# The first MoE's weight preparation spread over three engines, and batch 0's scores read from whole q and k

## The chip, the cores and the metric

The kernel runs on one core of one Trainium2 chip. The metric is device time in microseconds (us), as the median of several executions. The core has five engines that matter here: TensorE (PE in the rows, with PEld for its weight loads), VectorE (DVE), ScalarE (ACT), GpSimd (POOL) and SyncE (SP), whose queue issues most DMAs. Each engine works through its own instructions in the order in which they were written; an instruction that has to wait holds up everything behind it on that engine.

## The reference

Three stages follow one another: attention (the sum of a full attention over q, k and v averaged four by four, and of a local one in which a position sees the 3 before and the 3 behind it), a first MoE with one activation, and a second MoE with a product of two projections.

```python
    q_d = q.reshape(B, H, Sd, factor, D).mean(axis=3)      # k_d, v_d alike
    out_d = sm_attn(q_d, k_d, v_d)
    out_up = np.repeat(out_d, factor, axis=2)
    mask = np.abs(pos[:, None] - pos[None, :]) < factor
    ...
    out_local = np.matmul(attn, v)
    return (out_up + out_local).astype(np.float32)
...
    h = x @ w_in                # first MoE: 2304 x 512 by 512 x 2048
    r = np.maximum(h, 0.0)
    g = s * (r * r) + b
    return (g @ w_out).astype(np.float32)
...
    a = x @ w_a                 # second MoE: 512 x 1536, twice
    b = x @ w_b
    return (a * b @ w_out).astype(np.float32)
```

There are 4 batches of 576 positions, 8 heads of 64. The weights of both MoEs arrive as 64-bit floats.

## The kernel before, in words

**Order.** The kernel is a list of tasks. Each has an engine, a modelled duration, inputs, buffers that it takes and gives back, and a due time. `Program.order` (a list scheduler inside the kernel file) takes again and again the task that can start first, and among equals the one that is due first, and writes the instructions in that order. So the order of each engine's instructions is fixed when the kernel is built; on the chip only semaphores hold. `SEEN` is the modelled delay from the end of a task until another engine sees it. An engine named `GQ` stands for DMAs that GpSimd issues; in the emitted program these DMAs (line 541) are instructions of GpSimd's own stream. Due times are counted from `T0` and `STEP` (`target(idx)` is the due time of iteration idx of the first MoE) with the constants `DUE_...`.

**Attention, in four steps a part.** `down(b, hp)` is the averaged attention of batch b and head pair hp: q and k are loaded whole (128 x 576), averaged (line 572 on VectorE for batch 0, lines 574 and 575 on GpSimd for the others), scores on TensorE (L610), softmax on VectorE and ScalarE, transposes (L661), the product with the averaged v (L681). For batch 0, v is averaged by lines 595 and 596 on GpSimd; for the others `pool_in` sums it by DMAs that accumulate (L541), three for each half, each behind the one before. `tile_job(i)` is the local attention of 96 positions by TensorE (scores L760 on q and k loaded for the tile, transposes L810, product L828, sum with the upsampled part L842, split into high and low L493 and L497). Eight tiles, of positions 0 to 767, are done this way; the others are `unit`s of 128 positions, done on VectorE (L879 to L955).

**The ramp.** The first 768 positions (batch 0's and batch 1's `down`, eight tiles) and the weights of the first MoE are the ramp. Its buffers are one pool (`rp`). The pool of the units is opened only when all ramp tasks are written (`open_b`), and takes its memory over.

**Weights.** `w_slice(k)` makes one of 32 slices (128 x 512) of the first MoE's weights. The raw 64-bit words come by DMA into one of 33 shared slots `w`. ScalarE makes z from the upper words (L334) and three bits of the lower words (L345); VectorE puts the sign there (L350) and joins both (L358). Then the value is split into two parts: the high one is rounded by ScalarE (L374), the low one is the difference, by VectorE (L379). At most `MAX_STAGED` raw slices are in SBUF at a time. Line 345 has four forms: it reads 16-bit or 8-bit elements and writes 32-bit or 16-bit ones, by turns.

**First MoE.** 6 blocks of 384 positions, 16 iterations each, 96 iterations. One iteration is 12 matmuls into h (L1030 to L1032), three ScalarE passes (L1047, L1051, L1054), one VectorE subtraction (L1058) and 12 matmuls into acc (L1073 to L1075). Iteration f of block 0 needs weight slices 2f and 2f+1 and block 0's positions (tiles 0 to 3). Block 1 needs tiles 4 to 7, block 2 three units. Until the first of these matmuls the kernel fills gaps on TensorE with small matmuls (L266) that keep its clock up; behind it there are no fillers.

**Second MoE.** From about 541 us to the end, on the result of the first. Its weights go through the same lines 334 to 358.

Of the kernel before, what the change touches and what calls it, by code (L numbers as in the profile page):

```python
# [7 lines left out]
F32 = mybir.dt.float32  # L8
# [3 lines left out]
U8 = mybir.dt.uint8  # L12
# [55 lines left out]
RAMP_BUFS = {"dq": 1, "dk": 1, "dv": 2, "qd": 1, "kd": 1, "vp": 4, "tq": 2, "tk": 2, "tv": 2, "e": 1, "x": 1, "z": 2}  # L68
# [6 lines left out]
ENGINES = ("PE", "DVE", "ACT", "POOL", "SP", "GQ", "CTL")  # L75

SEEN = {"PE": 0.2, "DVE": 0.13, "ACT": 0.22, "POOL": 0.15, "SP": 2.0, "GQ": 2.5, "CTL": 0.0}


class Task:  # L80
    __slots__ = (
        "eng", "dur", "fn", "deps", "succ", "acq", "picks", "rel", "due", "lead", "share", "num", "left", "ready", "start",
        "end", "fill",
# [24 lines left out]
class Program:  # L108
# [8 lines left out]
    def add(self, eng, dur, fn, reads=(), writes=(), acq=(), rel=(), due=1e9, after=(), lead=0.0, share=1.0):  # L117
        t = Task()
        t.eng, t.dur, t.fn, t.acq, t.rel, t.due = eng, dur, fn, acq, rel, due
# [14 lines left out]
    def order(self):  # L134
        for t in reversed(self.tasks):
            for s in t.succ:
                t.due = min(t.due, s.due - s.dur - SEEN[t.eng])
# [17 lines left out]
        while len(out) < len(self.tasks):  # L155
# [49 lines left out]
            for a in t.rel:  # L205
                a = a(t) if callable(a) else a
                self.free[a].append(t.end + SEEN[t.eng])
            out.append((t, picks))
            for u in t.succ:
                u.left -= 1  # L210
                u.ready = max(u.ready, t.end + (0.0 if u.eng == t.eng == "PE" else SEEN[t.eng]))
# [15 lines left out]
def moe_chain(ctx, tc, qT, kT, vd, tq, tk, tv, qu, ku, vu, w_a1, w_o1, w_a2, w_b2, w_o2, sb, ident_d, bmask_d, emask_d, out):  # L227
# [85 lines left out]
    def w_words(k, spool, z, first, name, acq=(), after=()):  # L313
# [49 lines left out]
    def w_slice(k, ph, lo_eng, after=()):  # L363
# [1268 lines left out]
```

## Time and profile before

| | us |
|---|---|
| median of 3 executions | 978.01 |
| lowest, highest | 977.96, 978.42 |
| the profiled execution | 977.19 |
| its span, from the first to the last instruction | 975.4 |

The page shows one execution. Busy time is what an engine spent inside instructions; a wait of an engine is named with the instruction that ended it. The table by stretches gives busy time of each engine between two times, with the granted TensorE clock (1.00 is 2.4 GHz, 0.50 is 1.2 GHz). TensorE's busy time before about 85 us holds the fillers, so it says little there.

### The profile page before, as it was taken

To read this page: it belongs to the slowest core of one execution; us is meant where nothing else is said; L and a number is where in the kernel's file an instruction comes from. 1 tells how busy PE (TensorE), PEld (TensorE's weight loads), DVE (VectorE), ACT (ScalarE), POOL (GpSimd) and SP (SyncE) were. 2 spreads that over 40 slices of the span, in tenths; PEclk is the share of its full clock that TensorE was granted. 3 is DMA by queue.
4 is the path that set the end of the run, shared out by engine and by line. 5 is a ranking of instruction groups with operands and counts; after the bars stand their busy time and mean duration, and the time that the engine had idled before them with its cause. 6 is when DMAs were issued, how large, how long until landed. Compare 5 with 4: busy or idle time off the path is not lost.

```text
span 975.4 us, 14509 instructions
## 1 busy us (share of the span) xinstructions
PE 930.3 (95%) x5371; PEld 858.5 (88%) x5371; DVE 787.2 (81%) x1377; ACT 520.4 (53%) x1144; POOL 76.7 (8%) x86
## 2 busy tenths in 40 slices
PE   8589699999899999999999999999999999999997
PEld 4357699999799999999999999998999998999995
DVE  5378888899999999997776899978977779777753
ACT  3479999434444454434888756534533334533322
POOL 2440110202222120000000000000000000000000
PEclk9799799999799999999999999999999999999999
DMA  6676851623435342321456623100500000200001
GB/s 181 151 231 201 275 165 44 199 78 89 147 106 100 121 121 66 98 65 51 164 169 230 229 72 124 64 22 23 173 22 23 22 22 11 98 22 23 0 1 66
DMA packets 48159, 99.19 MB, mean 102 GB/s; under 512 B 6536, under 2 KB 22248, under 8 KB 47704
## 3 DMA queue, kind: packets, MB, share of 16 engines
q1 hardware_dynamic: 40888, 95.60, 29.9%
q0 software_dynamic: 7200, 2.67, 2.4%
q8 instruction: 42, 0.69, 0.3%
q14 instruction: 29, 0.24, 0.1%
HBM read 85.65 MB, written 12.58 MB: 101 GB/s over the span
## 4 chain that ended last, share of the span: by engine, by line
PE 79%; DVE 9%; ACT 5%; DMA 3%; issue 2%; POOL 1%; SPq 0%; ACTq 0%; POOLq 0%
PE ab L1304 26%; PE h L1030 6%; PE h L1032 6%; PE acc L1073 6%; PE h L1031 6%; PE acc L1074 6%; PE acc L1075 6%; PE acc L1446 5%; PE acc L1445 5%; PE acc L1444 5%; DMA pv<-in_vd_dram 2%; ACT w L345 1%; DVE pr L940 1%; DVE xo L1181 1%; PE sc L610 1%
## 5 line engine op out<-in xcount | busy, mean ns | idle before, releaser
L1304 PE MATMUL ab<-xo,w 128*128 128x384 f32 x1370 | 276.9, 339 | 1.0 <-DVE w L1334 0.5
L1304 PEld LDWEIGHTS ab<-xo,w 128*128 128x128 f32 x1370 | 246.7, 189 | 16.9 <-DVE u L1378 0.8
L1030 PE MATMUL h<-xsh,w 128*128 128x384 f32 x384 | 132.8, 346 | 1.6 <-ACT u L1047 0.8
L1073 PE MATMUL acc<-gh,w 128*128 128x384 f32 (+1 forms) x384 | 132.5, 345 | 0.5 <-ACT w L345 0.5
L1074 PE MATMUL acc<-gl,w 128*128 128x384 f32 x384 | 130.3, 339 | 0.7 <-DVE gl L1058 0.7
L1032 PE MATMUL h<-xsh,w 128*128 128x384 f32 x384 | 130.4, 340 | 0.2 <-DVE w L379 0.2
L1031 PE MATMUL h<-xsl,w 128*128 128x384 f32 x384 | 130.4, 340 | 0.0
L1075 PE MATMUL acc<-gh,w 128*128 128x384 f32 (+1 forms) x384 | 129.9, 338 | 0.0
L1047 ACT ACTIVATE u<-h 128x384 f32<-128x384 f32 x96 | 48.1, 501 | 123.2 <-PE h L1032 118.3
L1420 ACT ACTIVATE gh<-u 128x384 fp32r<-128x384 f32 x68 | 35.8, 526 | 90.5 <-DVE u L1381 54.4
L1030 PEld LDWEIGHTS h<-xsh,w 128*128 128x128 f32 x384 | 73.3, 191 | 4.8 <-issue 2.3
L1073 PEld LDWEIGHTS acc<-gh,w 128*128 128x128 f32 x384 | 72.5, 189 | 2.6 <-issue 1.3
L1074 PEld LDWEIGHTS acc<-gl,w 128*128 128x128 f32 x384 | 72.6, 189 | 1.6 <-DVE gl L1058 1.6
L1032 PEld LDWEIGHTS h<-xsh,w 128*128 128x128 f32 x384 | 73.2, 191 | 0.6 <-DVE w L379 0.6
L1031 PEld LDWEIGHTS h<-xsl,w 128*128 128x128 f32 x384 | 73.3, 191 | 0.0
L1075 PEld LDWEIGHTS acc<-gh,w 128*128 128x128 f32 x384 | 72.5, 189 | 0.0
L1058 DVE TENSOR_TENSOR gl<-u,gh 128x384 fp32r<-128x384 f32 x96 | 54.0, 562 | 16.8 <-ACT gh L1054 16.5
L1328 ACT ACTIVATE w<-ab 128x384 f32<-128x384 f32 x32 | 15.7, 491 | 92.9 <-PE ab L1304 89.0
L345 ACT ACTIVATE w<-w 128x512 int32<-128x512 uint8 (+3 forms) x63 | 63.6, 1025 | 0.0
L350 DVE TENSOR_SCALAR w<-w 128x512 uint16<-128x512 f32 x63 | 47.5, 765 | 14.2 <-ACT w L345 14.0
L1054 ACT ACTIVATE gh<-u 128x384 fp32r<-128x384 f32 x96 | 50.6, 528 | 2.4 <-PE acc L1075 0.4
L1051 ACT ACTIVATE u<-u 128x384 f32<-128x384 f32 x96 | 50.7, 528 | 1.9
(199 smaller groups left out, 1790.2 us busy)
## 6 DMA issues: line engine op xcount, KB each, us to landing
w<-in_w_o_dram SPq DMA_DIRECT2D x27, 512.0 KB
w<-in_w_a_dram SPq DMA_DIRECT2D x26, 512.0 KB
bk<-in_ku_dram SPq DMA_DIRECT2D x22, 320.0 KB
bk<-in_vu_dram SPq DMA_DIRECT2D x22, 320.0 KB
w<-wod SPq DMA_DIRECT2D x12, 512.0 KB
w<-in_w_b_dram SPq DMA_DIRECT2D x10, 512.0 KB
dk<-in_kT_dram SPq DMA_DIRECT2D x16, 288.0 KB
x2d<-ev SPq DMA_DIRECT2D x24, 192.0 KB
```

The source lines that it names most:

```text
L345: A_.activation(out=halves()[:, :, 0] if k % 2 else low, in_=src, func=ACTF.Copy, scale=scale, bias=bias)
L1030: nc.tensor.matmul(out=st["h"], lhsT=w[:, 0, k], rhs=hi[:, k], start=(k == 0), stop=False)
L1031: nc.tensor.matmul(out=st["h"], lhsT=w[:, 0, k], rhs=lo[:, k], start=False, stop=False)
L1032: nc.tensor.matmul(out=st["h"], lhsT=w[:, 1, k], rhs=hi[:, k], start=False, stop=(k == HP - 1))
L1051: A_.activation(out=st["u"], in_=st["u"], func=ACTF.Square)
L1054: A_.activation(out=st["hi"][:, :n], in_=st["u"], func=ACTF.Copy)
L1058: V.tensor_tensor(out=st["lo"], in0=st["u"], in1=st["hi"][:, :n].bitcast(F32), op=ALU.subtract)
L1073: nc.tensor.matmul(out=acc, lhsT=wh, rhs=st["hi"], start=(f == 0), stop=False)
L1074: nc.tensor.matmul(out=acc[:, :n], lhsT=wh, rhs=st["lo"], start=False, stop=False)
L1075: nc.tensor.matmul(out=acc, lhsT=wl, rhs=st["hi"], start=False, stop=(f == FA - 1))
L1304: nc.tensor.matmul(out=o, lhsT=w[:, k], rhs=x, start=(not more and k + n == 0), stop=(k == 1 and n == 2), skip_group_check=more,)
L1444: nc.tensor.matmul(out=acc, lhsT=gh, rhs=w[:, 0], start=first, stop=False)
```

## The change

1. **q and k of batch 0** are loaded into `w` slots (8 of them) and stay until all six tiles of batch 0 have their scores. These tiles read them there, and their own loads of q and k are gone (12 loads).
2. **v of batch 0** is averaged on VectorE (one reduction for each of 8 halves) instead of two GpSimd instructions each.
3. **The accumulating DMAs** belong to GpSimd in the scheduler, too, with 6.0 us until they are seen; `GQ` is gone. They and batch 1's `down` are due later.
4. **Line 345** has one form left: 16-bit in, 32-bit out. This holds for all 68 slices of both MoEs.
5. **High parts** of the first MoE's 32 slices go from ScalarE to VectorE (a copy); **every second low part** goes from VectorE to GpSimd.
6. `MAX_STAGED` is 5 instead of 3, buffer counts of the ramp, due times and leads are other numbers.

```diff
-W_ENG_A = ["DVE"]
+W_ENG_A = ["DVE", "POOL"]
+
+H_ENG_A = ["DVE"]
 DOWN_ENG = [("DVE", "DVE")] * 4
-MAX_STAGED = 3
+MAX_STAGED = 5
...
-T0, STEP = 36.0, 3.95 / 384
-LEAD = 20.0
-DUE_DOWN = (12.0, 2.5, 0.0, 8.0)
-DUE_TILE = (4.0, 5.0, 25.0)
-DUE_JOB = (14.0, 12.0, 15.0)
+T0, STEP = 28.8, 3.759 / 384
+LEAD = 10.0
+DUE_DOWN = (8.8, -5.0, 0.0, 8.0)
+DUE_NEXT = (46.5, 0.0)
+DUE_TILE = (12.1, 11.0, 18.5)
+DUE_JOB = (14.0, 19.5, 21.0)
...
-RAMP_BUFS = {"dq": 1, "dk": 1, "dv": 2, "qd": 1, "kd": 1, "vp": 4, "tq": 2, "tk": 2, "tv": 2, "e": 1, "x": 1, "z": 2}
+RAMP_BUFS = {"dq": 2, "dk": 2, "dv": 2, "qd": 1, "kd": 1, "vp": 4, "tq": 1, "tk": 1, "tv": 2, "e": 1, "x": 1, "z": 2}
...
-ENGINES = ("PE", "DVE", "ACT", "POOL", "SP", "GQ", "CTL")
-
-SEEN = {"PE": 0.2, "DVE": 0.13, "ACT": 0.22, "POOL": 0.15, "SP": 2.0, "GQ": 2.5, "CTL": 0.0}
+ENGINES = ("PE", "DVE", "ACT", "POOL", "SP", "CTL")
+
+SEEN = {"PE": 0.2, "DVE": 0.13, "ACT": 0.22, "POOL": 0.15, "SP": 2.0, "CTL": 0.0}
...
             low = st["low"] = words()[:, :, 0]
-            if k % 4 < 2:
-                src, scale, bias = halves()[:, :, 1], 2.0 ** -13, -4095.5 * 2.0 ** -13
-            else:
-                src = st["s"].rearrange("p a m -> p (a m)").bitcast(U8).rearrange("p (m c) -> p m c", c=8)[:, :, 3]
-                scale, bias = 2.0 ** -5, -15.5 * 2.0 ** -5
-            A_.activation(out=halves()[:, :, 0] if k % 2 else low, in_=src, func=ACTF.Copy, scale=scale, bias=bias)
-
-        add("ACT", 0.9, a_fn, [("st", k)], [("low", k)])
+
+            A_.activation(out=low, in_=halves()[:, :, 1], func=ACTF.Copy, scale=2.0 ** -13, bias=-4095.5 * 2.0 ** -13)
+
+        add("ACT", 0.56, a_fn, [("st", k)], [("low", k)])
...
-            A_.activation(out=wt[k][:, 0], in_=st["z"], func=ACTF.Copy)
-
-        add("ACT", 0.52, h_fn, [("t", k)], [("wh", k)], [("w",)])
+            if h_eng == "DVE":
+                V.tensor_copy(out=wt[k][:, 0], in_=st["z"])
+            else:
+                A_.activation(out=wt[k][:, 0], in_=st["z"], func=ACTF.Copy)
+
+        add(h_eng, 0.35 if h_eng == "DVE" else 0.52, h_fn, [("t", k)], [("wh", k)], [("w",)])
...
-        add(lo_eng, 1.23 if lo_eng == "POOL" else 0.61, l_fn, [("wh", k)], [("w", k)], rel=[ph + "z"])
+        add(lo_eng, 1.33 if lo_eng == "POOL" else 0.61, l_fn, [("wh", k)], [("w", k)], rel=[ph + "z"])
...
+    def wide_in(p):
+        return slot(p[0], F32).rearrange("p a m -> p (a m)")[:, :S]
...
-                    "GQ" if r else "SP", 1.3, fn, (), [("pv", b)] if r == 3 else (), () if r + kh else [("pv",)], (), due,
-                    [t[kh]] if r else [t[0]] if kh else after,
+                    "POOL" if r else "SP", 1.25, fn, (), [("pv", b)] if r == 3 else (), () if r + kh else [("pv",)], (), due,
+                    [t[kh]] if r else [t[0]] if kh else after, seen=6.0,
...
-            st["k"] = new(ph, "dk", [128, S])
+            st["k"] = whole["k", b, hp] = wide_in(p) if b == 0 else new(ph, "dk", [128, S])
...
-        load(l_q, 128 * HP * TQ * 4, writes=[("tq", i)], acq=[(names["tq"],)], after=after)
-        load(l_k, 128 * HP * TW * 4, writes=[("tk", i)], acq=[(names["tk"],)], after=after)
+        if b:
+            load(l_q, 128 * HP * TQ * 4, writes=[("tq", i)], acq=[(names["tq"],)], after=after)
+            load(l_k, 128 * HP * TW * 4, writes=[("tk", i)], acq=[(names["tk"],)], after=after)
+
+        k0, k1 = max(0, 3 - t0), min(TW, S + 3 - t0)
...
+                add("CTL", 0.0, free_fn, after=mm["whole"], rel=["w"] * 2 * HP)
...
-        down(0, hp, "r", DOWN_ENG[hp], "POOL", target(0) - DUE_DOWN[0] + DUE_DOWN[1] * hp)
+        down(0, hp, "r", DOWN_ENG[hp], "DVE", target(0) - DUE_DOWN[0] + DUE_DOWN[1] * hp)
...
-        w_slice(k, "r", W_ENG_A[k % len(W_ENG_A)])
-    pool_in(1, P.made["open", "r"], target(0))
+        w_slice(k, "r", H_ENG_A[k % len(H_ENG_A)], W_ENG_A[k % len(W_ENG_A)])
+    pool_in(1, P.made["open", "r"], target(FA) - DUE_NEXT[0])
     for hp in range(HP):
-        down(1, hp, "r", ("POOL", "POOL"), "POOL", target(0))
+        down(1, hp, "r", ("POOL", "POOL"), "POOL", target(FA) - DUE_NEXT[0] + DUE_NEXT[1] * hp)
```

## Rows read from the trace of the kernel before

**Rows 1.** The page's first part: busy time, share of the span, instructions, by engine.
```profile
PE 930.3 (95%) x5371; PEld 858.5 (88%) x5371; DVE 787.2 (81%) x1377; ACT 520.4 (53%) x1144; POOL 76.7 (8%) x86
```

**Rows 2.** Table by stretches: from:to, length, busy time of each engine, PEclk, DMA.
```profile
0.00:34.40 34.40, 26.35 (x190) 14.66 (x190) 18.74 (x46) 15.36 (x75) 9.81 (x17) 0.95 0.62 173
34.40:45.30 10.90, 4.27 (x28) 2.50 (x29) 0.01 (x1) 0.66 (x3) 6.68 (x10) 0.59 0.57 111
45.30:60.00 14.70, 10.64 (x97) 7.48 (x98) 8.63 (x19) 8.56 (x41) 5.87 (x9) 0.84 0.70 199
60.00:170.60 110.60, 100.17 (x721) 88.01 (x718) 93.97 (x187) 108.12 (x268) 15.12 (x14) 0.95 0.59 184
...
174.20:254.50 80.30, 75.18 (x444) 72.35 (x443) 77.64 (x107) 36.68 (x84) 13.51 (x13) 0.98 0.43 132
254.50:541.00 286.50, 286.31 (x1699) 277.94 (x1698) 247.97 (x373) 161.93 (x345) 25.76 (x25) 0.99 0.39 120
```

**Rows 3.** Waits from 0 to 60 us: who waited for whom, total, times, longest.
```profile
PE o L681 <- POOL vp L596: 13.9, 4, 7.7
```

**Rows 4.** GpSimd in order of time, 38 to 41 us: start, length, instruction.
```profile
38.02 1.21 POOL L541 DMA_DIRECT2D pv<-in_vd_dram  x1 [3.32 <-issue]
...
40.07 0.45 POOL L596 TENSOR_TENSOR vp<-dv 72x128 f32<-72x128 f32 x1
```

**Rows 5.** The accumulating DMAs, line 541, 0 to 180 us: issue to landing.
```profile
DMA to landing us min/median/max: 3.7/5.9/10.9
```

**Rows 6.** TensorE in order of time: first MoE's start, a stall, ends of blocks 0 and 1.
```profile
84.68 0.44 PE L1030 MATMUL h<-xsh,w 128*128 128x384 f32 x1
...
104.75 1.92 PE L828 MATMUL o<-w,tv 102*64 102x96 f32 x16 [6.81 <-ACT w L820]
...
107.81 0.52 PE L1031 MATMUL h<-xsl,w 128*128 128x384 f32 x1
108.13 0.52 PE L1032 MATMUL h<-xsh,w 128*128 128x384 f32 x1
...
170.08 0.33 PE L1032 MATMUL h<-xsh,w 128*128 128x384 f32 x1
...
253.01 0.67 PE L1030 MATMUL h<-xsh,w 128*128 128x384 f32 x1
```

**Rows 7.** VectorE in order of time: the last low part, the first unit.
```profile
169.90 0.69 DVE L379 TENSOR_TENSOR w<-z,w 128x512 fp32r<-128x512 f32 x1 [0.15 <-ACT w L374]
...
174.19 2.03 DVE L879 TENSOR_TENSOR pr<-bq,bk 128x1792 f32<-128x1792 f32 x1 [1.46 <-DMA bq<-in_qu_dram]
```

**Rows 8.** Groups of instructions by form: count, busy time, mean ns of one.
```profile
L345 ACT ACTIVATE w<-w 128x512 uint16<-128x512 uint8 x16 | 21.9, 1372 | 0.0
L379 DVE TENSOR_TENSOR w<-z,w 128x512 fp32r<-128x512 f32 x32 | 21.9, 691 | 1.4 <-ACT w L374 1.1
L374 ACT ACTIVATE w<-z 128x512 fp32r<-128x512 f32 x32 | 20.5, 648 | 0.3 <-DVE z L358 0.3
L345 ACT ACTIVATE w<-w 128x512 int32<-128x512 uint16 x15 | 10.3, 689 | 0.0
```

**Rows 9.** VectorE's two converting copies, in order of time.
```profile
4.87 0.32 DVE L293 CAST bmaskb<-tq 96x306 bf16<-96x306 f32 x1 [3.78 <-DMA tq<-in_bmask_dram]
...
11.41 0.21 DVE L288 CAST identb<-ident 96x96 bf16<-96x96 f32 x1 [1.94 <-DMA ident<-in_ident_dram]
```

**Rows 10.** GpSimd sums in order of time: two lengths, then one beside VectorE's work.
```profile
57.32 0.67 POOL L574 TENSOR_TENSOR dq<-dq 128x288 f32<-128x288 f32 x1
58.07 0.44 POOL L575 TENSOR_TENSOR qd<-dq 128x144 f32<-128x144 f32 x1
...
68.17 2.05 POOL L574 TENSOR_TENSOR dq<-dq 128x288 f32<-128x288 f32 x1
```

**Rows 11.** VectorE in order of time: one instruction alone, then beside GpSimd's sums.
```profile
46.51 1.00 DVE L802 TENSOR_TENSOR w<-w,tsm 96x816 f32<-96x816 f32 x1
...
50.98 1.72 DVE L802 TENSOR_TENSOR w<-w,tsm 96x816 f32<-96x816 f32 x1
```

More of the change, by code (lines that the diff above doesn't have):

```diff
@@ L11 @@
 I32 = mybir.dt.int32
-U8 = mybir.dt.uint8
 U16 = mybir.dt.uint16
@@ L82 @@
         "eng", "dur", "fn", "deps", "succ", "acq", "picks", "rel", "due", "lead", "share", "num", "left", "ready", "start",
-        "end", "fill",
+        "end", "fill", "seen",
     )
@@ L115, in __init__, with add @@
         self.free = {k: [0.0] * n for k, n in free.items()}
-    def add(self, eng, dur, fn, reads=(), writes=(), acq=(), rel=(), due=1e9, after=(), lead=0.0, share=1.0):
+    def add(self, eng, dur, fn, reads=(), writes=(), acq=(), rel=(), due=1e9, after=(), lead=0.0, share=1.0, seen=None):
         t = Task()
+        t.seen = SEEN[eng] if seen is None else seen
         t.eng, t.dur, t.fn, t.acq, t.rel, t.due = eng, dur, fn, acq, rel, due
@@ L136, in order @@
             for s in t.succ:
-                t.due = min(t.due, s.due - s.dur - SEEN[t.eng])
+                t.due = min(t.due, s.due - s.dur - t.seen)
         avail = {e: [] for e in ENGINES}
@@ L206, in order @@
                 a = a(t) if callable(a) else a
-                self.free[a].append(t.end + SEEN[t.eng])
+                self.free[a].append(t.end + t.seen)
             out.append((t, picks))
@@ L210, in order @@
                 u.left -= 1
-                u.ready = max(u.ready, t.end + (0.0 if u.eng == t.eng == "PE" else SEEN[t.eng]))
+                u.ready = max(u.ready, t.end + (0.0 if u.eng == t.eng == "PE" else t.seen))
                 if not u.left:
@@ L361, in w_words, with w_slice @@
         return tz
-    def w_slice(k, ph, lo_eng, after=()):
+    def w_slice(k, ph, h_eng, lo_eng, after=()):
         st = {}
@@ L527, in moe_chain @@
     pooled = {}
+    whole = {}
+    def wide_in(p):
+        return slot(p[0], F32).rearrange("p a m -> p (a m)")[:, :S]
     def pool_in(b, after, due):
@@ L555, in l_k @@
         def l_k(p):
-            st["k"] = new(ph, "dk", [128, S])
+            st["k"] = whole["k", b, hp] = wide_in(p) if b == 0 else new(ph, "dk", [128, S])
             return st["k"], kT[b, hp]
         def l_q(p):
-            st["q"] = new(ph, dq, [128, S])
+            st["q"] = whole["q", b, hp] = wide_in(p) if b == 0 else new(ph, dq, [128, S])
             return st["q"], qT[b, hp]
-        load(l_k, 128 * S * 4, writes=[("dk", key)], acq=[(ph + "dk",)], after=after)
-        load(l_q, 128 * S * 4, writes=[("dq", key)], acq=[(ph + dq,)], after=after)
+        load(l_k, 128 * S * 4, writes=[("dk", key)], acq=[("w",) if b == 0 else (ph + "dk",)], after=after)
+        load(l_q, 128 * S * 4, writes=[("dq", key)], acq=[("w",) if b == 0 else (ph + dq,)], after=after)
         for name, src in (("k", "dk"), ("q", "dq")):
@@ L578, in down @@
                 eng, dve(S) if eng == "DVE" else 1.25, prep, [(src, key)], [(name + "d", key)],
-                [(ph + name + "d",)], [ph + (dq if src == "dq" else src)],
+                [(ph + name + "d",)], [ph + (dq if src == "dq" else src)] if b else (),
             )
@@ L745, in l_v, with qk @@
             return st["v"], tv[i]
-        load(l_q, 128 * HP * TQ * 4, writes=[("tq", i)], acq=[(names["tq"],)], after=after)
-        load(l_k, 128 * HP * TW * 4, writes=[("tk", i)], acq=[(names["tk"],)], after=after)
+        if b:
+            load(l_q, 128 * HP * TQ * 4, writes=[("tq", i)], acq=[(names["tq"],)], after=after)
+            load(l_k, 128 * HP * TW * 4, writes=[("tk", i)], acq=[(names["tk"],)], after=after)
+        k0, k1 = max(0, 3 - t0), min(TW, S + 3 - t0)
+        def qk(name, hp):
+            if b:
+                return st[name][:, hp] if name == "q" else st[name][:, hp, k0:k1]
+            w = whole[name, b, hp]
+            return w[:, t0:t0 + TQ] if name == "q" else w[:, t0 - 3 + k0:t0 - 3 + k1]
         load(l_v, TW * DM * 4, writes=[("tv", i)], acq=[(names["tv"],)], after=after)
@@ L760, in s_fn @@
                     nc.tensor.matmul(
-                        out=sc[h][:, hp], lhsT=st["q"][h * D:h * D + D, hp], rhs=st["k"][h * D:h * D + D, hp],
+                        out=sc[h][:, hp, k0:k1], lhsT=qk("q", hp)[h * D:h * D + D], rhs=qk("k", hp)[h * D:h * D + D],
                         start=False, stop=(hp == HP - 1),
@@ L765, in tile_job, with free_fn @@
         ts = add(
-            "PE", 1.75, s_fn, [("tq", i), ("tk", i), "const"], [("tsc", i)], [wide, wide, E_SLOT[ph]],
-            [names["tq"], names["tk"]], after=[mm["dS", b, hp] for hp in range(HP)], lead=LEAD, share=0.55,
-        )
+            "PE", 1.75, s_fn, ([("tq", i), ("tk", i)] if b else [(x, (0, hp)) for x in ("dk", "dq") for hp in range(HP)]) + ["const"],
+            [("tsc", i)], [wide, wide, E_SLOT[ph]], [names["tq"], names["tk"]] if b else (),
+            after=[mm["dS", b, hp] for hp in range(HP)], lead=LEAD, share=0.55,
+        )
+        if b == 0:
+            mm.setdefault("whole", []).append(ts)
+            if len(mm["whole"]) == S // TQ:
+                def free_fn(p):
+                    pass
+                add("CTL", 0.0, free_fn, after=mm["whole"], rel=["w"] * 2 * HP)
         def m_fn(p):
```

## The prediction

> **What bounds the kernel now.** I read the page's first part, then the table by stretches, then the waits of the first 60 us, and only then single instructions. The first part says that TensorE is busy for 95% of the span [rows 1], but its fillers count in that, so the table is the better view [rows 2]. From 254.5 to 541 us TensorE is busy 286.3 of 286.5 us: nothing can be won there but TensorE work, and the change takes none away. Before that three things are to be seen. From 34.4 to 45.3 us VectorE has 0.01 us of work and ScalarE 0.66, and the clock falls to 0.59: the whole ramp stands. From 60 to 170.6 ScalarE is busy 108.1 of 110.6 us (98%), VectorE 94.0 (85%): ScalarE sets the pace of the weights. From 174.2 to 254.5 VectorE is busy 77.6 of 80.3 us: it makes the three units on which block 2 waits.
>
> The standstill has a name. TensorE waits four times, 13.9 us in all, for line 596, the averaged v that GpSimd makes [rows 3]. In GpSimd's order that instruction stands behind an accumulating DMA that runs only at 38.0; v is done at 40.5 [rows 4]. These DMAs land 3.7 to 10.9 us after their issue, median 5.9 [rows 5], and each waits for the one before on the engine that also owes v to TensorE. The scheduler put them on an engine of their own, which the program does not have.
>
> The first MoE's matmuls start at 84.68, and block 0's last h ends at 170.4 [rows 6]. VectorE makes the last low part at 169.90 and only then starts the first unit, at 174.19, because the units' pool opens behind all of the ramp [rows 7]. Block 2 starts at 253.0 [rows 6], one VectorE stretch later. So the end of the ramp, pushed along by VectorE's full stretch and then by TensorE's full one, sets the end of the kernel. A microsecond off the ramp is a microsecond off the total.
>
> **The change part by part.** ScalarE in the ramp: 32 high parts of 648 ns leave it, 20.7 us. Of line 345's 32 instructions there, 16 write 16-bit elements at 1372 ns; they become the form of 689 ns, 16 x 0.68 = 10.9 us [rows 8]. That is 31.6 us of instruction lengths; busy time counts where two overlap once, so I take 25 us as the safe end. ScalarE stops being the bound: 108.1 less 25 is 83 us of 110.6. The other half of line 345 is in the second MoE, where TensorE is the bound; I count it at nothing, since TensorE's full stretch hides it.
>
> VectorE in the ramp: it is busy 18.7 + 0.0 + 8.6 + 94.0 = 121.4 us up to 170.6, and idle 49.2 [rows 2]. Sixteen low parts go: 16 x 0.69 = -11.0 us [rows 8]. The copies come: no copy of 512 elements is in the trace. The two converting copies took 0.32 us for 306 elements and 0.21 for 96 [rows 9], 0.52 ns an element, so 512 take 0.21 + 416 x 0.00052 = 0.43 us (an estimate), 13.7 us for 32. If the rounding copy runs at the rate of a subtraction it is 0.69 us, 22.1 us in all [rows 8]. I take 0.43, since a copy is nearer to a copy. Eight v averages come, each a reduction over 512 elements; a subtraction of 512 takes 0.69 us [rows 8], and at that rate they are 5.5 us.
>
> Sixteen low parts come to GpSimd. Its sums took 0.67 us for 288 elements and 0.44 for 144 with VectorE out of the way [rows 10], 1.6 ns an element, so 512 take about 1.0 us; beside VectorE's work the same 288 elements took 2.05 us [rows 10]. That is 16 to 50 us in a ramp of 150, on an engine that was busy 37.5 us up to 170.6 [rows 2] and drops sixteen v sums: it has room. What they cost VectorE is the open price. A product of two operands on VectorE went from 1.00 to 1.72 us beside GpSimd's sums [rows 11]; elsewhere it was GpSimd that waited, as in the 2.05 us. I take half of the 0.72, rounded down to 0.3 us for each of 16, 5 us, with 0 and 16 (each one holds VectorE for its whole 1.0 us) as the ends.
>
> Work for VectorE: 121.4 - 11.0 + 13.7 + 5.5 + 5 = 134.6 us. The ends are 128 (no contention) and 152 (slow copies, full contention).
>
> Idle time of VectorE: of the 49.2 us, the 10.9 of the standstill go, since v is now made where its consumers' other inputs are made, and about 4 of the 6.1 from there to 60 us go with them (6.2 of TensorE's 13.9 us for line 596 are outside its longest wait [rows 3]). Of the 15.7 idle up to 34.4, 5 are the first loads; with q and k no longer queued for one buffer each and five raw slices let in instead of three, weights can fill some of it. I keep 14 of these 17.8. From 60 on 16.6 were idle beside a full ScalarE; an engine that is the bound is held 98% busy by this kind of order, as ScalarE shows [rows 2], so I keep 4. Idle together 18, with 8 and 26 as ends.
>
> The ramp then ends at 134.6 + 18 = 152.6 instead of 170.6: 18.0 us earlier. TensorE can follow: it does the last 64 iterations and the rest of its attention in 286.5 us [rows 2], at most 4.5 us an iteration, so block 0 takes at most 72 us. What is late next is VectorE itself, in the ramp and then in the units; its stretch of 80 us before block 2 stays, and behind that TensorE's.
>
> Other edits. The twelve loads that go (tiles 0 to 5) free queue time on SyncE; the waits of the first 60 us name no such load as TensorE's releaser, so I count nothing beyond the idle time above. Eight `w` slots are held until the sixth tile's scores; of 33 slots that leaves 25 for weights, more than are ready by then, and if it did not, weight loads would wait on SyncE's queue and loads behind them as well. The accumulating DMAs are still instructions of GpSimd: each waits there for the one before, and low parts and batch 1's averages are queued behind it. With 6.0 us planned and 5.9 the median landing [rows 5], the wait is about nothing; at 10.9 it is 4.9 us for each of six, 29 us of GpSimd time, of which only a low part needed within that time reaches TensorE. The other due times, leads and buffer counts change the order alone; I have no row that prices them and let the range carry them, 5 us to either side.
>
> The sum against the profiled execution is 977.2 - 18.0 = 959.2; the median of the runs shown is 0.8 us above that execution, so 960.0.
>
> **The rivals.** (a) The ramp shrinks further. VectorE's low end with 8 us idle is 128 + 8 = 136, the ramp ends 34.6 us earlier, and the time is 943. For it speaks that no single engine was full before 60 us [rows 2]; against it that TensorE, VectorE and ScalarE hand each tile to and fro, and each hand-over waits. I give its whole region, 943 to 952, 0.20.
>
> (b) GpSimd holds VectorE up. Each of the 16 low parts shuts VectorE out for its whole length: 16.5 us instead of 5, and the time is 971.5; with a landing at 10.9 us in front of a needed low part it is up to 976. For it speaks the stretched product [rows 11], against it the sum of 2.05 us [rows 10]: there GpSimd waited. The chance is 0.17. The Trainium skill, "SBUF — State Buffer", section "Who interferes with whom", has a rule for this: VectorE and GpSimd share a port pair that the first to start holds for its whole instruction, and copies and instructions with two SBUF inputs want it. The product of [rows 11] agrees, with 0.72 us lost; by the rule alone the sum would be that of this rival.
>
> (c) Slower: a starved TensorE loses its clock. In block 0 there are no fillers. At 104.75 TensorE had waited 6.81 us, and its matmuls then followed one another every 0.32 us [rows 6], the 1.2 GHz level. If a MoE that starts 18 us earlier, at 66.7, runs ahead of its weights and stays at that level, an iteration takes 24 x 0.32 = 7.7 us, block 0 ends at 66.7 + 123 = 189.7 instead of 170.4, and the time is 997. It decides from the point where some 60% of block 0 is at the low level: (170.4 - 66.7) / 16 = 6.5 us an iteration, between 4.5 and 7.7. Against it speaks that the clock was at 0.95 from 60 to 170.6 [rows 2] although the weights were late there, too. The chance is 0.08.
>
> (d) No change: VectorE's high end, 152 us of work, with 18 idle ends the ramp at 170, where it ended before. For this both unknown prices must be at their ends. The chance is 0.05, with 978 as the time.
>
> **How the numbers follow.** The forecast, 952 to 967 (a shift of 11 to 26 us), has 0.50; (a) 0.20, (b) 0.17, (c) 0.08, (d) 0.05. The range that leaves out 2 in 10 runs from 944, nearly all of (a), to 972, some half of (b). A measurement of this kernel can tell about 0.2%, 2 us, from no change. Faster by more: 0.50 + 0.20 + 0.17 = 0.87; the same 0.05; slower 0.08.
>
> **What would show it.** After: no wait of TensorE for v; no stretch of 10 us without VectorE work; ScalarE below 85% in the ramp and some 477 us in all (520.4 [rows 1] less 20.5, less 10.9, less 12.2 for 18 of the second MoE's 36 slices); VectorE 795 to 810 us; line 345 in one form near 0.69 us; the copy near 0.43 us; the last low part near 152; block 2 near 235; TensorE full from there on, and about 722 us from block 2's start to the end, as before. The prediction is wrong if the last low part comes later than 161, if the copy takes 0.69 us, or if block 2's start does not move with the ramp's end.

## The result and the profile after

The changed kernel takes 950.6 us (median of 4 executions, 949.4 to 953.3), against 978.1 for the kernel before (4 executions): a ratio of 0.972 with an interval of 0.970 to 0.9745, faster by 27.4 us. The profiled execution took 949.8 us, its span 948.0. The forecast was 960.0, 944 to 972, so the time lies in the range, but in the region that the prediction gave to rival (a).

The first part of the page after:

```profile
PE 913.0 (96%) x5330; PEld 844.9 (89%) x5330; DVE 799.9 (84%) x1401; ACT 483.7 (51%) x1112; POOL 96.5 (10%) x86
```

It answers to [rows 1]. VectorE has 799.9 us of work (forecast 795 to 810), ScalarE 483.7 (forecast some 477), GpSimd 96.5 instead of 76.7.

The table by stretches of the kernel after, cut at the first unit's start, at the end of block 2's first h, and at the end of the first MoE; the columns are those of [rows 2]:

```profile
0.00:153.86 153.86, 131.01 (x994) 104.95 (x995) 136.31 (x274) 109.86 (x353) 60.26 (x48) 0.98 0.65 186
153.86:228.50 74.64, 74.64 (x448) 73.10 (x447) 72.42 (x97) 31.44 (x70) 10.49 (x13) 1.00 0.41 121
228.50:514.30 285.80, 284.21 (x1709) 276.22 (x1708) 252.88 (x387) 159.14 (x360) 25.74 (x26) 1.00 0.43 129
514.30:948.00 433.70, 423.16 (x2185) 390.62 (x2183) 338.26 (x645) 183.27 (x330) 0.00 (x0) 1.00 0.15 51
```

The same table of the kernel before, cut at the same events:

```profile
0.00:174.19 174.19, 145.02 (x1050) 116.25 (x1051) 121.99 (x253) 134.10 (x385) 37.47 (x48) 0.92 0.61 178
174.19:258.70 84.51, 79.39 (x461) 75.30 (x461) 81.71 (x111) 36.98 (x86) 13.51 (x13) 0.96 0.43 129
258.70:540.80 282.10, 281.91 (x1681) 274.80 (x1682) 243.74 (x368) 161.49 (x343) 25.76 (x25) 0.99 0.39 121
540.80:975.40 434.60, 423.96 (x2185) 392.19 (x2183) 339.77 (x648) 187.79 (x331) 0.00 (x0) 0.99 0.15 53
```

The four differences are -20.3, -9.9, +3.7 and -0.9 us, together -27.4, the difference of the two spans. Two things stand out. The ramp shrank about as forecast (the first unit starts at 153.86, not 174.19). The stretch behind it, which the prediction had left as it was, shrank as well. In that stretch TensorE is now busy 74.64 of 74.64 us at a granted clock of 1.00, where before it was busy 79.39 of 84.51 at 0.96.

The waits of the first 160 us after (who waited for whom, total, times, longest):

```profile
POOL pv L549 <- DMA pv<-in_vd_dram: 28.2, 6, 15.6
...
ACT z L337 <- POOL w L381: 14.8, 8, 2.7
...
PE o L689 <- DVE vp L601: 5.5, 4, 2.2
...
PE sc L618 <- POOL qd L583: 3.6, 2, 2.1
```

The longest of GpSimd's own waits, in order of time:

```profile
16.09 1.32 POOL L549 DMA_DIRECT2D pv<-in_vd_dram  x1 [15.65 <-DMA pv<-in_vd_dram]
```

The standstill of [rows 3] is gone, but not to nothing: TensorE still waits 5.5 us for the averaged v, now made by VectorE, where it waited 13.9. The accumulating DMAs hold GpSimd for 28.2 us in all, but 15.6 of them lie before 16.09, where its first accumulating DMA waits for the plain load that it adds to. The other five waits are 12.6 us, well below the prediction's upper bound of 29. TensorE waits twice, 3.6 us, for batch 1's averaged q, which stands behind these DMAs in GpSimd's order. And there is a new wait that the prediction did not have: ScalarE waits eight times, 14.8 us, for a low part on GpSimd, because z has two buffers and GpSimd holds one of them.

### The profile page after: what moved, and what is told of

The parts are those of the page before. It is cut to its first block, busy times and chain, and to the rows that moved or that the text cites. A ratio compares the mean times of both kernels' runs of the same rounds, so it can differ in the third digit from the quotient of the medians.

```text
span 948.0 us, 14366 instructions
## 1 busy us (share of the span) xinstructions
PE 913.0 (96%) x5330; PEld 844.9 (89%) x5330; DVE 799.9 (84%) x1401; ACT 483.7 (51%) x1112; POOL 96.5 (10%) x86
## 4 chain that ended last, share of the span: by engine, by line
PE 66%; DVE 22%; issue 4%; DMA 3%; ACT 2%; POOL 2%; SPq 0%; DVEq 0%; ACTq 0%; POOLq 0%
PE ab L1331 25%; PE acc L1472 5%; PE acc L1473 5%; PE acc L1471 5%; PE acc L1100 4%; PE h L1057 4%; PE acc L1101 4%; PE acc L1102 4%; PE h L1059 4%; PE h L1058 4%; DVE pr L906 2%; DVE z L357 2%; DVE w L349 2%; DVE gl L1085 1%; DVE pr L967 1%
## 5 line engine op out<-in xcount | busy, mean ns | idle before, releaser
L1331 PE MATMUL ab<-xo,w 128*128 128x384 f32 x1252 | 265.8, 338 | 1.5 <-DVE w L1361 1.2
L1331 PEld LDWEIGHTS ab<-xo,w 128*128 128x128 f32 x1252 | 225.0, 188 | 17.9 <-DVE w L1361 1.8
L1331 PE MATMUL ab<-xo,wx 128*128 128x384 f32 x260 | 71.1, 337 | 0.0
L1355 ACT ACTIVATE w<-ab 128x384 f32<-128x384 f32 x31 | 15.2, 490 | 88.2 <-PE ab L1331 78.8
L349 DVE TENSOR_SCALAR w<-w 128x512 uint16<-128x512 f32 x64 | 49.8, 789 | 5.7 <-ACT w L344 5.7
L906 DVE TENSOR_TENSOR pr<-bq,bk 128x1792 f32<-128x1792 f32 (+1 forms) x26 | 49.8, 1915 | 3.2 <-DMA bq<-in_qu_dram 2.8
```

Of the source, the lines that this page charges most:

```text
L349: V.tensor_scalar(out=halves()[:, :, 1], in0=words()[:, :, 1].bitcast(F32), scalar1=0.0, scalar2=32768.0, op0=ALU.is_lt, op1=ALU.mult)
L906: V.tensor_tensor(out=pr, in0=st["q", h].unsqueeze(2).to_broadcast([128, R, 7, D]), in1=window(st["k", h], R), op=ALU.mult,)
L1331: nc.tensor.matmul(out=o, lhsT=w[:, k], rhs=x, start=(not more and k + n == 0), stop=(k == 1 and n == 2), skip_group_check=more,)
```

## The experiments

All ratios are to the kernel before, with their 95% interval. In the text "ramp end" is the start of the first unit.

**1. The change without its new division of high and low parts.** High parts go back to ScalarE, all low parts to VectorE; everything else is as in the kernel after.

```
-W_ENG_A = ["DVE", "POOL"]
+W_ENG_A = ["DVE"]
-H_ENG_A = ["DVE"]
+H_ENG_A = ["ACT"]
```

> The changed kernel with its title part undone: the 32 high parts on ScalarE again, all 32 low parts on VectorE. If VectorE's work sets the ramp's length: it loses the copies (15 us) and the excess of some 12 us that its instructions show beside GpSimd's sums, and gets 16 low parts (11 us), so some 16 us less of 136; ScalarE gets 20.7 us, which brings it to about 98% in the middle of the ramp. Ramp end between 142 and 150 instead of 152, time 941 to 950. If ScalarE was the true bound of the ramp: the ramp ends at 158 or later, time 956 to 962.

Measured: 948.0 us, 0.9698 (0.9676 to 0.9719). That is 2.6 us less than the kernel after, with intervals that overlap: the division is worth nothing here, or less than nothing. VectorE's work in the ramp falls to 123.95 us and the ramp ends at 145.09 (table by stretches):

```profile
0.00:145.09 145.09, 131.20 (x970) 106.12 (x971) 123.95 (x257) 122.16 (x382) 30.77 (x32) 0.94 0.69 198
...
145.09:224.10 79.01, 79.01 (x472) 77.34 (x471) 76.60 (x108) 35.18 (x83) 9.14 (x13) 1.00 0.41 123
```

The time and the ramp's end are as expected for a ramp that VectorE's work sets. The second row shows why only 4.4 of the 8.8 us that the ramp gained are still there at the end of block 2's first h: TensorE is busy in all of the 79.01 us. It runs 472 instructions there, 24 more than after. VectorE's earlier end of the ramp here uncovers work that TensorE still had to do.

**2. High parts on VectorE, but no low part on GpSimd.**

```
-W_ENG_A = ["DVE", "POOL"]
+W_ENG_A = ["DVE"]
```

> The changed kernel with every low part on VectorE, high parts still on VectorE. If what GpSimd takes off VectorE (16 x 0.69 = 11 us) is given back by VectorE's instructions that stand still beside GpSimd's sums (about 12 us over the ramp), the time is the same within 4 us: 947 to 955. If GpSimd's help is real: VectorE has 11 us more, 960 or more. If the contention costs more than it shows: under 945.

Measured: 943.6 us, 0.9652 (0.9631 to 0.9673), 7.1 us less than the kernel after, and the fastest of all that ran. This is the third of the expected cases. The rows of its ramp and of the way to the end of block 2's first h, and one wait of its ramp:

```profile
0.00:147.32 147.32, 134.38 (x994) 108.99 (x995) 132.23 (x290) 109.56 (x353) 33.26 (x32) 0.94 0.68 195
147.32:222.10 74.78, 74.78 (x448) 73.10 (x447) 72.55 (x97) 31.48 (x71) 10.90 (x13) 1.00 0.41 120
```

```profile
ACT z L337 <- DVE w L381: 8.1, 11, 1.7
```

VectorE makes sixteen more low parts and yet has 132.23 us of work instead of 136.31. So leaving sixteen low parts to GpSimd costs VectorE more time than making them itself. ScalarE's waits for a buffer z fall from 17.0 us (14.8 of them for GpSimd) to 8.1. The ramp ends 6.5 us earlier than in the kernel after, and behind it nothing is lost again: the way to the end of block 2's first h has the same 448 instructions of TensorE in 74.78 us.

**3. Batch 0's v on GpSimd again**, in the kernel after.

```
-        down(0, hp, "r", DOWN_ENG[hp], "DVE", target(0) - DUE_DOWN[0] + DUE_DOWN[1] * hp)
+        down(0, hp, "r", DOWN_ENG[hp], "POOL", target(0) - DUE_DOWN[0] + DUE_DOWN[1] * hp)
```

> The changed kernel with batch 0's averaged v on GpSimd as before, the accumulating DMAs still counted as GpSimd's own work in the scheduler. If the engine of v removed the standstill: TensorE waits for v again by 5 us or more in total, a stretch without VectorE work of several us returns, time 957 to 965. If it was the scheduler's knowledge of the DMAs: v stands ahead of them in GpSimd's order, VectorE saves 8 us, time 945 to 952.

Measured: 957.5 us, 0.9794 (0.9772 to 0.9817), 6.8 us more than after; the ramp ends at 163.9 instead of 153.9. TensorE's longest sum of waits in that ramp:

```profile
PE sc L618 <- POOL qd L583: 8.7, 3, 4.6
```

It is no longer v that TensorE waits for but batch 1's averaged q, which stands behind v in GpSimd's order. What GpSimd has to do late comes out at TensorE one way or another.

**4. Batch 0's v on VectorE alone**, in the kernel before.

```
-        down(0, hp, "r", DOWN_ENG[hp], "POOL", target(0) - DUE_DOWN[0] + DUE_DOWN[1] * hp)
+        down(0, hp, "r", DOWN_ENG[hp], "DVE", target(0) - DUE_DOWN[0] + DUE_DOWN[1] * hp)
```

> The kernel before with one thing changed: batch 0's v is averaged on VectorE. If the standstill comes from v behind the accumulating DMAs on GpSimd: TensorE's 13.9 us of waits for v go, the ramp ends some 14 us earlier and ScalarE, 98% busy from 60 us on, stays the bound; first unit at 158 to 163, time 962 to 968. If other work of GpSimd behind the same DMAs (batch 1's averages) holds TensorE up as soon as v does not: less than half of it, time 971 or more.

Measured: 966.1 us, 0.9898 (0.9861 to 0.9934), 12 us faster. The time is that of the first expected case, but the path is not: the ramp ends at 171.6, only 2.6 us earlier (ScalarE is busy 133 us of it), and of TensorE's waits in it the longest is now this one:

```profile
PE sc L610 <- POOL qd L575: 9.4, 1, 9.4
```

The rest of the gain lies behind the ramp, in the way to block 2 (74.9 us instead of 84.5). Experiment 9 says what happened there.

**5. The scheduler told where the accumulating DMAs run**, in the kernel before: they become GpSimd's, seen after 6.0 us.

```
-                    "GQ" if r else "SP", 1.3, fn, (), [("pv", b)] if r == 3 else (), () if r + kh else [("pv",)], (), due,
-                    [t[kh]] if r else [t[0]] if kh else after,
+                    "POOL" if r else "SP", 1.25, fn, (), [("pv", b)] if r == 3 else (), () if r + kh else [("pv",)], (), due,
+                    [t[kh]] if r else [t[0]] if kh else after, seen=6.0,
...
```

> The kernel before with one thing changed: the scheduler counts the accumulating DMAs as GpSimd's work, seen after 6.0 us. If the wrong model of that queue made the standstill: v is written ahead of the DMAs or between them without a hold, TensorE's wait for v falls below 5 us, time 962 to 970. If the engine has to change because DMAs and sums share one queue: the wait stays above 8 us, time 974 to 980.

Measured: 965.3 us, 0.9867 (0.9847 to 0.9888), 12.9 us faster. Nearly all of it is in the ramp, which ends at 162.54, 11.7 us earlier (table by stretches):

```profile
0.00:162.54 162.54, 144.23 (x1030) 115.64 (x1031) 123.65 (x252) 133.52 (x385) 37.43 (x48) 0.93 0.66 191
162.54:247.00 84.46, 79.57 (x462) 75.49 (x461) 79.66 (x108) 37.02 (x85) 13.65 (x13) 0.95 0.43 130
```

With the same work on the same engines, v comes in time (TensorE waits 3.2 us for it). The way to block 2 stays at 84.46 us, with a busy TensorE of 79.57, as before.

**6. The division of the weight work alone**, in the kernel before: high parts on VectorE, every second low part on GpSimd, one form of line 345.

```
-W_ENG_A = ["DVE"]
+W_ENG_A = ["DVE", "POOL"]
...
-            A_.activation(out=wt[k][:, 0], in_=st["z"], func=ACTF.Copy)
+            V.tensor_copy(out=wt[k][:, 0], in_=st["z"])
...
```

> The kernel before with the split of the weight work alone: high parts on VectorE, every second low part on GpSimd, line 345 in one form. v stays on GpSimd. If ScalarE was the bound from 60 to 170 us and the standstill stays: ScalarE has 25 to 31 us less, VectorE some 15 us more (94 + 15 of 110), so VectorE takes over as the bound and little is won, 968 to 978; the wait for v, and low parts behind it, could even cost, 980. If ScalarE's relief counts in full: 955 to 962.

Measured: 990.2 us, 1.0124 (1.0099 to 1.015): slower, by 12 us, and outside everything that was expected. Its ramp in the table by stretches, and the waits in it from 30 us on:

```profile
0.00:194.04 194.04, 146.85 (x1013) 114.77 (x1014) 133.30 (x266) 110.60 (x353) 60.69 (x64) 0.86 0.56 160
```

```profile
ACT z L334 <- POOL w L374: 28.4, 12, 15.2
...
PE o L823 <- ACT w L815: 15.7, 1, 15.7
...
PE o L676 <- POOL vp L591: 12.5, 3, 8.1
```

The work falls from ScalarE as the prediction has it (110.6 us instead of 134.1), but the ramp becomes 20 us longer. A low part in GpSimd's order stands behind an accumulating DMA, which waits for the one before it; meanwhile it holds one of two buffers z, ScalarE stands, and TensorE waits 15.7 us for ScalarE. GpSimd in order of time shows one such case:

```profile
102.99 1.19 POOL L536 DMA_DIRECT2D pv<-in_vd_dram  x1 [7.42 <-DMA pv<-in_vd_dram]
103.74 1.75 POOL L374 TENSOR_TENSOR w<-z,w 128x512 fp32r<-128x512 f32 x1
```

So the part of the change on which the prediction's sum rests most gives nothing by itself; where the scheduler does not see what holds GpSimd up, it costs.

**7. The new due times and leads alone**, in the kernel before, and **8. the old ones**, in the kernel after (the same lines the other way round).

```
-T0, STEP = 36.0, 3.95 / 384
-LEAD = 20.0
+T0, STEP = 28.8, 3.759 / 384
+LEAD = 10.0
...
```

> The kernel before with the changed kernel's due times and lead alone (batch 1's sums and averages due later, too). If the numbers do nothing as long as GpSimd's queue stands in the way: 972 to 982. If they take the accumulating DMAs out of the way of v by making them due later, or shorten the way from the first unit to block 2: 962 to 970.

> The changed kernel with the due times and the lead of the kernel before (T0, STEP, LEAD, DUE_DOWN, DUE_TILE, DUE_JOB; batch 1's own due time set back to that of the first iteration). If the numbers only order equals: within 4 us of 950.6. If the 8 to 10 us that the way from the first unit to block 2 became shorter come from them: that way is 79 us again instead of 71, TensorE waits before block 2, time 958 to 964.

Measured: alone 976.8 us, 0.999 (0.9975 to 1.0006), no change that can be told; taken away from the kernel after, 954.4 us, 0.9774 (0.9748 to 0.98), 3.7 us more than after, hardly clear of its interval, with the ramp end at 159.8. The numbers bring little, and only to a program whose queues are in order. The way to block 2 is 74.5 us in the kernel after with the old numbers, so the kernel after doesn't need the new ones for it. But the way alone does not tell the time: in the profiled execution of experiment 7 (973.2 us, the fastest of ten) it is 77.8 us, 6.7 shorter than before, and from its end to the end of the kernel 6.1 us more go by (722.9 instead of 716.7).

**9. Only the order ahead of block 2**, in the kernel before: batch 2's second scores are written behind the transposes of block 2's third unit.

```
+        mm["bt", u] = tb
...
+    late, early = mm["dS", 2, 1], mm["bt", 2]
+    late.deps.append(early)
+    early.succ.append(late)
```

> The kernel before with one dependency more: the scores of batch 2's second averaged attention stay behind the third unit's transposes in TensorE's order. The ramp is untouched (first unit at 174). If block 2 was late because those transposes waited for PSUM banks that these scores held until VectorE and ScalarE had dealt with them: block 2's first iteration ends 8 to 12 us earlier (247 to 251 instead of 258.7), time 966 to 970. If the way from the first unit to block 2 is VectorE's work whatever the order: 976 to 980.

Measured: 969.3 us, 0.9911 (0.9892 to 0.993), 9.3 us faster, and all of it behind the ramp (table by stretches):

```profile
0.00:174.21 174.21, 147.13 (x1049) 117.33 (x1050) 122.54 (x253) 133.95 (x385) 37.12 (x48) 0.91 0.61 179
174.21:248.10 73.89, 72.72 (x434) 70.46 (x433) 71.46 (x91) 31.58 (x69) 10.15 (x12) 1.00 0.41 120
```

The ramp end is the same to 0.02 us; the way to block 2 falls from 84.51 to 73.89 us, what the kernel after has (74.64). This shows where the second gain of the change came from; the next section reads it.

**10. Line 345's four forms**, in the kernel after.

```
-            A_.activation(out=low, in_=halves()[:, :, 1], func=ACTF.Copy, scale=2.0 ** -13, bias=-4095.5 * 2.0 ** -13)
+            if k % 4 < 2:
...
+            A_.activation(out=halves()[:, :, 0] if k % 2 else low, in_=src, func=ACTF.Copy, scale=scale, bias=bias)
```

> The changed kernel with line 345's four forms of before. ScalarE gets some 11 us in the ramp and 12 us in the second MoE. If ScalarE is no longer a bound in the changed kernel: 948 to 954. If its work still counts one for one in the ramp: 958 or more.

Measured: 956.5 us, 0.9784 (0.9759 to 0.9808), 5.9 us more than after. This lies between what the two expected. ScalarE has 118.3 us of a ramp of 157.7, so it is not full, and the longer forms still cost something: the ramp ends 3.9 us later.

**11. q and k of batch 0 loaded anew for each tile**, in the kernel after, with buffers of their own again (two each for the whole q, the whole k and the tiles', where the kernel before has one each for the whole ones).

```
-            st["k"] = whole["k", b, hp] = wide_in(p) if b == 0 else new(ph, "dk", [128, S])
+            st["k"] = new(ph, "dk", [128, S])
...
-        if b:
-            load(l_q, 128 * HP * TQ * 4, writes=[("tq", i)], acq=[(names["tq"],)], after=after)
+        load(l_q, 128 * HP * TQ * 4, writes=[("tq", i)], acq=[(names["tq"],)], after=after)
...
```

> The changed kernel with batch 0's q and k in buffers of their own (two each) and loaded a second time for the six tiles, as before. If the twelve loads cost nothing beyond queue time: 947 to 955. If holding q and k in SBUF is what fills VectorE's idle time at the start: the ramp ends 6 us or more later, 956 to 965.

Measured: 957.9 us, 0.9791 (0.9773 to 0.9809), 7.2 us more than after; the ramp ends at 162.0, 8.1 us later, with about the same work on every engine (table by stretches):

```profile
0.00:162.02 162.02, 137.89 (x1018) 109.93 (x1019) 138.86 (x277) 109.28 (x353) 59.56 (x48) 0.97 0.65 190
```

**12. All low parts on VectorE, high parts on VectorE and ScalarE by turns**, in the kernel after.

```
-W_ENG_A = ["DVE", "POOL"]
+W_ENG_A = ["DVE"]
-H_ENG_A = ["DVE"]
+H_ENG_A = ["DVE", "ACT"]
```

> The changed kernel with all low parts on VectorE and the high parts by turns on VectorE and ScalarE. With high parts on VectorE alone it was busy 132 us of a ramp of 147, with all of them on ScalarE 124 of 145. If the two bounds only need to be balanced: VectorE about 128, ScalarE about 115, ramp 142 to 146, time 939 to 944. If the order, not the work, sets the rest: 943 to 950.

Measured: 946.9 us, 0.9672 (0.9644 to 0.9701). It has less work for VectorE than experiment 2 (129.6 us instead of 132.2), but its ramp ends at 152.0 instead of 147.3 and its time is no better. The mere balance of VectorE and ScalarE no longer decides at this point.

## Why the prediction was right, and where it was not

**The place of the gain: right, and ScalarE is no longer the bound.** Everything gained lies ahead of block 2. From block 2's start to the end the kernel took 721.8 us after (226.21 to 948.0) against 722.4 before (253.01 [rows 6] to 975.4); the prediction said about 722. ScalarE is busy 69.6 of the 93.9 us from 60 us to the ramp end, 74%, below the 85% that was asked for.

**The ramp: right in the sum, by terms of which several were off and cancelled.** Forecast were 134.6 us of work for VectorE and 18 idle up to the end of the last low part, at 152.6. It ends at 150.54, and VectorE's work up to there is 135.8 us, its idle time 14.7. Of that 10.6 us lie before 60 us (forecast 14) and 4.1 behind (forecast 4):

```profile
0.00:150.54 150.54, 127.69 (x975) 101.63 (x976) 135.82 (x273) 108.76 (x350) 60.26 (x48) 0.98 0.65 186
```

The groups by form in the first 160 us after, to be held against [rows 8]:

```profile
L381 POOL TENSOR_TENSOR w<-z,w 128x512 fp32r<-128x512 f32 x16 | 29.0, 1810 | 50.6 <-DVE w L374 24.2 <-ACT w L681 8.2 <-ACT u L1078 7.9
...
L344 ACT ACTIVATE w<-w 128x512 int32<-128x512 uint16 x32 | 21.3, 682 | 0.1
...
L374 DVE CAST w<-z 128x512 fp32r<-128x512 f32 x32 | 15.2, 490 | 0.2
...
L381 DVE TENSOR_TENSOR w<-z,w 128x512 fp32r<-128x512 f32 x16 | 12.0, 750 | 0.1
...
L829 DVE TENSOR_TENSOR w<-w,tsm 96x816 f32<-96x816 f32 x6 | 8.5, 1420 | 0.1
...
L601 DVE TENSOR_REDUCE vp<-dv 72x128 f32<-72x512 f32 x8 | 8.2, 1029 | 1.5 <-DMA dv<-in_vd_dram 1.5
```

- The copy: forecast 0.43 us, measured 0.43 undisturbed and 0.49 in the mean, 15.2 us instead of 13.7. The choice of the copies' row over the subtraction's was right.
- The v averages: forecast 0.69 us each, measured 1.03, 8.2 us instead of 5.5. The row of a subtraction was too far from a reduction.
- A low part on GpSimd: forecast 1.0 us, measured 1.29 to 3.63, in the mean 1.81, 29 us in all, inside the 16 to 50.
- What they cost VectorE: forecast 5 us, ends 0 and 16. I summed, over VectorE's instructions that ran beside a GpSimd sum, their length above the median of the same form with GpSimd at rest: 16.0 us after, 3.0 before, 3.5 in experiment 2. So the price is 13 us, 0.8 for each low part and not 0.3, near the upper end. This is rival (b)'s mechanism, and it is there.
- What made up for these: the sum added instruction lengths. On a full engine each instruction starts a little before the end of the one before (the row at 132.92 below starts 0.10 us before its predecessor ends). The groups' lengths of VectorE's ramp add up to 157.9 us after and 135.1 before, 22.8 more, while its busy time grew by 14.3. The other 8.5 us are overlap, which the prediction counted for ScalarE ("busy time counts where two overlap once") and forgot for VectorE.

VectorE in order of time, after, with two of the places where it loses time, and then GpSimd in the same time:

```profile
132.86 0.16 DVE L1087 CAST gh<-ones 128x2 fp32r<-128x2 f32 x1
132.92 0.69 DVE L357 SCALAR_TENSOR_TENSOR z<-z,w 128x512 int32<-128x512 int32 x1
...
134.53 1.78 DVE L357 SCALAR_TENSOR_TENSOR z<-z,w 128x512 int32<-128x512 int32 x1
136.34 0.43 DVE L374 CAST w<-z 128x512 fp32r<-128x512 f32 x1
...
140.58 1.52 DVE L374 CAST w<-z 128x512 fp32r<-128x512 f32 x1
```

```profile
134.20 1.56 POOL L381 TENSOR_TENSOR w<-z,w 128x512 fp32r<-128x512 f32 x1 [2.24 <-ACT u L1074]
140.27 1.54 POOL L381 TENSOR_TENSOR w<-z,w 128x512 fp32r<-128x512 f32 x1 [4.51 <-DVE w L374]
...
149.24 1.30 POOL L381 TENSOR_TENSOR w<-z,w 128x512 fp32r<-128x512 f32 x1 [2.28 <-ACT u L1078]
```

Line 357 takes 0.69 us at 132.92 and 1.78 at 134.53, a third of a microsecond after GpSimd's low part began at 134.20; the copy takes 0.43 us at 136.34 and 1.52 at 140.58, again a third behind GpSimd. Each lost 1.09 us, about what GpSimd had left (1.23 us in both cases). The rule on the shared port pair that the prediction names (the Trainium skill, "SBUF — State Buffer", section "Who interferes with whom") agrees with these rows. By that rule alone it would be every low part's whole length; measured is half of it, 0.8 of 1.55 us (the median). Why it is half is not shown: of nine copies that ran beside a low part or another GpSimd sum, seven kept 0.41 or 0.42 us, and two lost about a microsecond.

**The step that failed: "its stretch of 80 us before block 2 stays".** It named VectorE's units as the bound there. From the first unit to block 2's start it was 78.8 us before (174.19 to 253.01) and 72.3 after (153.86 to 226.21), and the low clock behind it, some 3 us more up to the end of block 2's first h, went too. Block 2's start moved by 26.8 us where the ramp's end moved by 20.3. This failed step is why the time came out 9.4 us below the forecast of 960.0: 6.5 of it are this shorter stretch, 2.3 the ramp (20.3 instead of 18.0), 0.6 the rest. The stretch was not VectorE's alone. TensorE before, in order of time:

```profile
239.97 0.71 PE L610 MATMUL sc<-kd,qd 64*72 64x144 f32 x8
...
249.26 0.66 PE L970 MATMUL bt<-ident,o 128*128 128x128 f32 x4 [1.16 <-ACT e L637]
...
252.12 1.15 PE L661 MATMUL at<-ident,e 72*72 72x72 f32 x8 [2.20 <-DVE s L906]
```

VectorE before in the same time, and then ScalarE:

```profile
245.78 2.02 DVE L879 TENSOR_TENSOR pr<-bq,bk 128x1792 f32<-128x1792 f32 x1
247.72 0.63 DVE L627 TENSOR_SCALAR nb<-nb 72x4 f32<-72x4 f32 x1
```

```profile
248.38 0.38 ACT L637 ACTIVATE e<-sc,nb 72x144 f32<-72x144 f32 x1 [0.58 <-DVE nb L627]
```

Batch 2's scores are computed at 239.97, and the third unit's transposes, for which block 2 waits, come behind them at 249.26. The transposes wait for ScalarE's exp (line 637), which takes the scores out of PSUM; the exp waits for line 627 on VectorE; and that stands behind products of the fourth unit (245.78), which nobody needs yet. TensorE is idle for 4.0 us between 241.96 and 253.00, and then its clock falls (table by stretches, before):

```profile
241.96:253.00 11.04, 7.03 (x42) 6.17 (x42) 11.01 (x19) 6.45 (x18) 4.42 (x4) 0.93 0.65 208
253.00:261.50 8.50, 8.50 (x36) 6.87 (x35) 7.77 (x11) 2.53 (x6) 1.41 (x3) 0.50 0.16 43
```

8.5 us at 0.50 (1.2 GHz) are 4.2 us lost there. They are not found again at the end, though: from block 2's start on the kernel takes 722.4 us with this low clock and 721.8 after without it, 722.8 in experiment 9 without it and 721.7 in experiment 5 with it. Behind block 2's first h the kernel after runs 28 more instructions on TensorE up to the end of the first MoE (1709 instead of 1681), and 1.6 us idle instead of 0.2. After, the same two steps on TensorE stand the other way round, and block 2 follows without a gap (TensorE in order of time):

```profile
219.89 0.60 PE L997 MATMUL bt<-ident,o 128*128 128x128 f32 x4
...
223.36 0.71 PE L618 MATMUL sc<-kd,qd 64*72 64x144 f32 x8
...
226.21 0.34 PE L1057 MATMUL h<-xsh,w 128*128 128x384 f32 x1
```

Experiment 9 makes this one exchange in the kernel before and gets the whole difference of the way. Experiments 4 and 6 (74.9 and 74.6 us) have the exchanged order, too, although they share no edit; experiment 5 keeps the stall, at 84.46. So it is a by-product: the list scheduler writes the whole order anew with each edit, and in some orders the stall does not arise. That it is gone in the kernel after is luck; no part of the change aimed at it. The rows for it were there before the prediction: the matmul at 253.01 in [rows 6] took 0.67 us, the one at 84.68 there 0.44, and I read the former only as block 2's start.

**"What is late next is VectorE itself, in the ramp and then in the units": half wrong.** After, TensorE is busy 74.64 of the 74.64 us behind the ramp, VectorE 72.42. Both are near their end, but TensorE has no gap. "A microsecond off the ramp is a microsecond off the total" still holds a little further, in experiment 2: its ramp ends 6.5 us earlier than after, and its span is 6.1 us shorter (941.9). In experiment 1 it does not: the ramp ends 8.8 us earlier, and 4.4 of them go to work that TensorE still had to do; its span is 4.7 us shorter (943.3).

**Edits counted at nothing.** The twelve tile loads, together with the place where q and k lie, are worth 7 us (experiment 11); the prediction had "nothing beyond the idle time above" for the loads. TensorE's waits named no such load. Loads and buffers were not separated, so which of them keeps the ramp back stays open. The due times are worth 3.7 us in the new program and nothing in the old one (experiments 7 and 8), within the 5 us that were allowed.

**The division of the weight work, on which the sum leans most: not borne out.** The prediction let ScalarE's relief of 25 us shorten the ramp. On the kernel before it alone makes the ramp 20 us longer (experiment 6); in the kernel after, taking it back costs nothing that can be told (experiment 1), and taking back its GpSimd half gains 7 us (experiment 2). Of the relief only the one form of line 345 shows a gain (5.9 us, experiment 10). So it is in part luck that the ramp came out near the forecast: moving the high and low parts did not shorten it, and edits that the sum counted at nothing did. What carried the gain is mostly the order: GpSimd's stream known to the scheduler (12.9 us alone, experiment 5), v away from it (6.8 us, experiment 3), whole q and k (7.2 us, experiment 11), one form of line 345 (5.9 us, experiment 10), and the freed stall (9.3 us, experiment 9). These overlap and do not add up to 27.4.

**The rivals.** (a) described the size (950.6 in 943 to 952), by another mechanism than its own: VectorE's work was 135.8 us and not at its low end of 128, and its idle time 14.7 and not 8. (b)'s mechanism is real, 13 us of VectorE's time, but it did not set the time by itself. (c) did not come: the clock in the ramp is 0.98 after, against 0.92 before. (d) did not come either.

**What stays open.** Why single edits move the ramp by just 4 to 8 us (experiments 8, 10 and 11): each rewrites the order of all engines, and work and order were not separated there. Nor is it known how much of experiment 2's 7 us is VectorE's lost time and how much ScalarE's wait for z, nor why the low clock at block 2's start is not found again at the kernel's end.

## What to carry to other kernels

Before work is moved between engines, look at what stands in the order of the engine that gets it: a queue whose waits the scheduler does not know (here DMAs in GpSimd's stream) turns a relief of 25 us into a loss of 12, and putting that one entry right gained as much without moving any work. In a stretch with a full VectorE, look also for idle rows and low-clock rows of TensorE before calling the stretch VectorE's; an instruction that nobody needs yet, ahead of one that frees a PSUM buffer, costs a wait, and the clock can fall behind it (here to 0.50 for 8.5 us). And GpSimd is no free third engine for elementwise work beside a full VectorE: with all low parts on VectorE and the rest of the change kept, the kernel takes 943.6 us, 0.9652 of the time before (0.9631 to 0.9673), faster than both kernels of this case.

## What the runs showed of the hardware

Even a copy of two elements can lose over a microsecond beside a GpSimd sum. VectorE after, the longest of sixteen (their median is 158 ns), while a GpSimd low part of 3.63 us runs from 98.22 to 101.85:

```profile
100.60 1.27 DVE L1087 CAST gh<-ones 128x2 fp32r<-128x2 f32 x1
```

TensorE waits for it: the first acc matmul of an iteration stands behind this cast, 4.1 us in five waits in the ramp. VectorE's reductions did not lose anything: of line 632's sixteen, four ran beside a GpSimd sum and took 0.44 to 0.45 us, as the others did (446 ns in the mean, as for line 624 before). And the reduction of v, 512 elements on 72 partitions that are read with a stride, took 1.03 us, longer than the one of q, 576 elements on 128 partitions that lie together (0.74 us).
